# Softmax reads and a softplus MLP on one core: the reads of six batches joined in three pairs, with a new order of steps and new homes

## The chip, the cores and the metric

The kernel runs on one core of a Trainium2 chip. The metric is the device time of one execution in microseconds (us); lower is better. The core's engines are TensorE (PE, matrix products; PEld is its weight load), VectorE (DVE), ScalarE (ACT) and GpSimdE (POOL, all but unused here). SyncE (SP) issues nearly all DMAs. Each engine takes its instructions in the order in which the program gives them, and a wait holds back all that stands behind it on that engine.

## The reference

```python
B, H, S, Ns, D = (8, 8, 512, 32, 64)
...
    scores = scale * np.matmul(x, state.transpose(0, 1, 3, 2))
...
    xread = np.matmul(a, state)        # a = softmax(scores)
    scores2 = scale * np.matmul(state, x.transpose(0, 1, 3, 2))
...
    sread = np.matmul(a2, x)           # a2 = softmax(scores2)
    return np.concatenate([xread, sread], axis=2).astype(np.float32)
...
    x = np.ascontiguousarray(attn_out.transpose(0, 2, 1, 3)).reshape(B * S, H * D)
...
    h = x @ w_in                       # 512 -> 2048
    g = np.maximum(h, 0.0) + np.log1p(np.exp(-np.abs(h)))
    return (g @ w_out).astype(np.float32)
```

Each of 8 batches and 8 heads has 512 rows x and 32 rows state, 64 wide. The x rows read the states (xread) and the states read the x rows (sread). The 8 x 544 rows that come out, 512 wide, go through a two-layer MLP with a softplus between.

## The kernel before

The program is a graph of named steps. Each has an engine or a choice of two, inputs, outputs and a function that emits its instructions. `PLAN` is a long table with one entry for each step, `name:engine:homes`, and is walked from its first entry to its last: it sets the order on every engine and the place of every tile. Engine letters are T (TensorE), A and C (ScalarE), V and W (VectorE) and S (a DMA queued on SyncE). Homes are numbers of PSUM banks (0 to 7) or of pages in one SBUF arena; a new tile in a page waits until the last work on the old tile is done, and where that is a store to DRAM, until the store has landed.

The steps that matter here, b being the batch:

- **Reads, `B.R…`** (function `read`): `sread` of a batch before its division by the row sums. 32 small products in tiles of 128 x 32 with 64 columns (64 records in the trace, for each is two), from `aT.b`, the transposed exponentials (four loads `Le.b.0` to `.3` from the DRAM buffer `te`), and `x.b` (two loads `Lx.b.0` and `.1` of 512 KB from `in_xn_dram`), into the PSUM tile `rp.b`. Behind it come the scaling `X.b`, a transpose `T.b` on TensorE (tile `tp`) and a split into two tiles that only the very last batch of states needs. All other large products use the whole array, in tiles of 128 x 128.
- **First product of the MLP, `h.b.f`**: for batch b and 128 of the 2048 columns, six products of 512 columns (L335, tile `h`). Softplus on ScalarE follows (`s…`, L717).
- **Second product**: for batch 0 plain, `m.0.f.c` (L335, tile `acc`, three products of 512 columns each); for the others in a form with fewer products, `p.b.s.u.j`, with banks `pk_X`, `pk_Y`, `pk_Z` (L764, six products of 256 columns to a step) and `pk_Q`, `pk_W` (L760 and L761).
- **Splits**: every operand is a sum of a high and a low part. ScalarE casts the high part (`wh`, `gh`, `vh`, L316) and VectorE subtracts for the low part (`wl`, `gl`, `vl`, L332). The w_out tiles for `m.0.f` are built from a load `Lo.f` by `ch.o f` on ScalarE (L367 or L369), `cu.o f` and `cr.o f` on VectorE (L374, L377, L382), and then split into `wh.f` and `wl.f`.
- **Spills**: softplus tiles of later batches are stored to `td` in DRAM (`Td…`, 512 KB) and loaded back (256 KB). SyncE issues these among the loads.

`GROUPS` names what one step of TensorE takes in a visit. The engine changes its tile shape where such a step begins and ends, 28 visits in small tiles in all, eight of them reads:

```python
    for name in GROUPS:
        parts = [{"V": states, "Q": scores, "R": read, "K": stacked}[u[0]](*map(int, u[1:].split("."))) for u in name.split("+")]
        op("B." + name, "T", list(dict.fromkeys(t for p in parts for t in p[0])), [t for p in parts for t in p[1]],
           lambda e, parts=parts: [p[2]() for p in parts])
```

Of the kernel before, what the change touches and what calls it, by code (L numbers as in the profile page):

```python
# [19 lines left out]
B, H, S, NS, D = 8, 8, 512, 32, 64  # L20
# [13 lines left out]
GROUPS = ('Q0', 'Q1', 'V1.0', 'V0.1+V1.1', 'V0.2+V1.2', 'V0.3+V1.3', 'Q2+Q3', 'V2.0+V3.0', 'V2.1+V3.1', 'V2.2+V3.2', 'V2.3+V3.3', 'K0.0', 'K0.1', 'K0.2', 'K0.3', 'K1.0', 'K1.1', 'K1.2', 'K1.3', 'K2.0', 'K2.1', 'K2.2', 'K2.3', 'K3.0', 'K3.1', 'K3.2', 'K3.3', 'Q4', 'Q5', 'Q6', 'Q7', 'R0', 'R1', 'R2', 'R3', 'R4', 'R5', 'R6', 'R7')  # L34
# [11 lines left out]
Lt.0.0:S:54 Lt.0.1:S:60 Lz.0:S:71 B.Q0:T:7,2 qk.0.0:A:86 qk.0.1:V:43 w.0:T:0 w.1:T:0 A.0.0:T:7 A.0.1:T:1 Li.0.0:S:56 ch.0.0:A:55 cu.0.0:V:66 cr.0.0:V: M.0.0:V:  # L46
M.0.1:V: Ms.0.0:V:28 Li.0.1:S:82 Lt.1.0:S:10 Lz.1:S:87 Lt.1.1:S:12 Ms.0.1:V:50 cu.0.1:V:0 m.0.0:A: ch.0.1:A:74 m.0.1:A: Lo.1:S:2 Li.0.2:S:24 Lo.0:S:8
Li.0.3:S:32 N.0.0:V: cr.0.1:V: w.2:T:0 w.3:T:0 B.Q1:T:7,2 V.0.0.0.1:T:4,5 V.0.0.0.0:T: Nm.0.0:V: qk.1.0:A:68 ch.o1:A:45 qk.1.1:A:41 A.1.0:T:6 D.0.0:T:1
A.1.1:T:3 N.0.1:V: Nm.0.1:V: D.0.1:T:2 vf.0.0:A:26 vf.1.0:A:64 ch.0.2:A:94 ac.0.1:A:63 ac.0.0:V:21 h.0.1.0:T:7 h.0.0.0:T:0 h.0.1.1:T: h.0.0.1:T: cu.o1:V:10
cr.o1:V: wh.1:A:96 ch.o0:A:34 ch.0.3:A:3 s.0.1:A:4 cu.0.2:V: M.1.0:V: cr.0.2:V: cu.0.3:V: cu.o0:V:79 cr.0.3:V: cr.o0:V: M.1.1:V: Ms.1.0:V:20 V.0.0.1.0:T:  # L50
V.0.0.1.1:T: vf.1.1:V: Ms.1.1:V:45 wl.1:V: vf.0.1:A: B.V1.0:T:1,2 s.0.0:A:46 gh.0.1:A:28 wh.0:A:50 gh.0.0:A:30 h.0.2.0:T:7 h.0.2.1:T: vh.1.0.0:A:52 s.0.2:A:32
Lo.2:S:54 Li.2.3:S:6 Li.1.1:S:60 Lo.3:S:8 ch.o2:C:38 gh.0.2:A:76 Li.1.2:S:82 Sq.1.1:S: Li.1.0:S:18 Lz.2:S:56 Li.1.3:S:24 Li.2.0:S:88 Li.3.2:S:14 Li.2.2:S:34
Li.2.1:S:92 Sq.0.1:S: Li.3.1:S:40 wl.0:V: gl.0.1:V: gl.0.0:V: h.0.3.0:T:3 h.0.3.1:T: s.0.3:A:12 cu.o2:W:69 gl.0.2:V: cr.o2:V: cu.o3:V:85 vl.1.0.0:V: m.1.0:A:
# [905 lines left out]
```

## Time and profile before

| | |
|---|---|
| median of 3 runs | 614.17 us (613.66 to 614.19) |
| the profiled execution | 615.17 us, of which its span 613.4 us and 1.77 us outside it |
| TensorE busy | 604.7 us (99% of the span) |
| VectorE busy | 517.6 us (84%) |
| ScalarE busy | 377.8 us (62%) |
| DMA | 141.04 MB, 230 GB/s mean |
| TensorE's granted clock | 1.00 in every slice |

The span is the time from the first to the last instruction that the profiler recorded; the time of the whole execution lies a little above it. A row of the timeline gives a start, a time, an engine, a line of the program, and how many instructions of one kind follow each other without a gap. TensorE's products overlap: each starts before the one ahead has ended, so the spacing of starts tells more than the duration.

### The profile page before, as it was taken

The page shows a single profiled execution, that of the slowest core. Times are in us where ns is not written, and L with a number is a line of the kernel's source. Part 1 is how long each engine was busy: PE and PEld are TensorE (multiplying, and loading weights), DVE is VectorE, ACT ScalarE, POOL GpSimd, SP SyncE. Part 2 cuts the span into 40 slices and gives each one's busy share as a digit, 9 for nine tenths or more (in the row PEclk, how much of TensorE's full clock was granted, in tenths as well). Part 3 has the DMA queues.
Part 4 walks back from the last instruction along what each step waited for, and adds up shares of the span by engine and source line. Part 5 has one row for each costly group of instructions (what it writes and reads, how often), then busy time and mean ns, then how long its engine had stood idle before and what let it go on. Part 6 is the DMA issues. An engine that isn't in the chain of part 4 may idle for free.

```text
span 613.4 us, 12010 instructions
## 1 busy us (share of the span) xinstructions
PE 604.7 (99%) x4452; PEld 519.5 (85%) x4452; DVE 517.6 (84%) x1117; ACT 377.8 (62%) x631; POOL 0.7 (0%) x6
## 2 busy tenths in 40 slices
PE   7999999999999999999999999999999999999997
PEld 4577667578878989999889998999988899999997
DVE  4999699788799999989699987899785788888974
ACT  4989798898576558674655644465444544546431
POOL 0000000000000000000000000000000000000000
PEclk9999999999999999999999999999999999999999
DMA  8977589988756877988896897874737782441303
GB/s 335 330 279 280 208 294 341 339 274 319 228 179 224 257 254 243 288 260 302 277 311 220 234 294 249 252 252 149 220 123 232 236 287 91 136 155 52 87 2 104
DMA packets 71418, 141.04 MB, mean 230 GB/s; under 512 B 7360, under 2 KB 17600, under 8 KB 71360
## 3 DMA queue, kind: packets, MB, share of 16 engines
q1 hardware_dynamic: 71072, 139.62, 68.7%
q8 instruction: 35, 0.57, 0.4%
q10 hardware_dynamic: 288, 0.66, 0.3%
q14 instruction: 23, 0.19, 0.1%
HBM read 83.10 MB, written 57.15 MB: 229 GB/s over the span
## 4 chain that ended last, share of the span: by engine, by line
PE 71%; DVE 3%; DMA 1%; ACT 1%; SPq 1%; issue 0%; ACTq 0%
PE h L335 14%; PE pk_X L764 14%; PE pk_Y L764 14%; PE pk_Z L764 7%; PE pk_Q L760 4%; PE h L818 2%; PE pk_Q L761 2%; PE pk_W L760 2%; PE pk_Z L760 2%; PE acc L335 1%; PE rp L335 1%; DMA td<-arena 1%; PE h L819 1%; PE pk_Z L761 1%; PE pk_W L761 1%; DVE arena L332 1%
## 5 line engine op out<-in xcount | busy, mean ns | idle before, releaser
L316 ACT CAST arena<-arena 128x896 fp32r<-128x896 f32 (+2 forms) x255 | 186.9, 760 | 137.1 <-DVE arena L745 27.3
L332 DVE TENSOR_TENSOR arena<-arena,arena 128x896 fp32r<-128x896 f32 (+2 forms) x255 | 212.8, 856 | 52.1 <-ACT arena L316 50.6
L335 PE MATMUL h<-arena,arena 128*128 128x512 f32 x760 | 187.0, 397 | 0.0
L335 PEld LDWEIGHTS h<-arena,arena 128*128 128x128 f32 x760 | 139.1, 188 | 38.2 <-issue 4.9
L764 PE MATMUL pk_X<-arena,arena 128*128 128x256 f32 x720 | 103.3, 284 | 0.0
L764 PE MATMUL pk_Y<-arena,arena 128*128 128x256 f32 x720 | 103.1, 283 | 0.0
L764 PEld LDWEIGHTS pk_X<-arena,arena 128*128 128x128 f32 x720 | 93.7, 190 | 4.0 <-issue 0.8
L764 PEld LDWEIGHTS pk_Y<-arena,arena 128*128 128x128 f32 x720 | 93.7, 190 | 3.5 <-issue 0.8
L717 ACT ACTIVATE arena<-h 128x512 f32<-128x512 f32 x112 | 64.4, 601 | 21.1 <-PE h L335 17.2
L764 PE MATMUL pk_Z<-arena,arena 128*128 128x256 f32 x360 | 52.1, 284 | 0.0
L742 DVE TENSOR_TENSOR arena<-arena 128x256 f32<-128x256 f32 x120 | 48.6, 417 | 2.1 <-DMA arena<-td 1.1
L764 PEld LDWEIGHTS pk_Z<-arena,arena 128*128 128x128 f32 x360 | 47.5, 190 | 1.5
L335 PE MATMUL acc<-arena,arena 128*128 128x512 f32 x192 | 45.7, 393 | 0.9 <-DVE arena L332 0.9
L760 PE MATMUL pk_Q<-arena,arena 128*128 128x512 f32 x112 | 43.9, 400 | 0.0
L335 PEld LDWEIGHTS acc<-arena,arena 128*128 128x128 f32 x192 | 35.6, 188 | 8.8 <-DVE arena L332 1.3
L744 DVE TENSOR_TENSOR arena<-arena 128x128 f32<-128x128 f32 x120 | 33.7, 285 | 1.1
L745 DVE TENSOR_TENSOR arena<-arena 128x128 f32<-128x128 f32 x120 | 32.7, 284 | 1.0
L761 PE MATMUL pk_Q<-arena,arena 128*128 128x256 f32 x112 | 31.4, 281 | 0.0
L332 DVE TENSOR_TENSOR arena<-vp,arena 128x512 fp32r<-128x512 f32 x30 | 20.0, 684 | 6.0 <-ACT arena L316 5.8
L760 PEld LDWEIGHTS pk_Q<-arena,arena 128*128 128x128 f32 x112 | 21.2, 189 | 3.3 <-issue 0.8
L818 PE MATMUL h<-sreadT,arena 128*128 128x512 f32 x64 | 22.8, 393 | 0.0
L760 PE MATMUL pk_W<-arena,arena 128*128 128x512 f32 x56 | 22.1, 398 | 0.0
(104 smaller groups left out, 648.3 us busy)
## 6 DMA issues: line engine op xcount, KB each, us to landing
td<-arena SPq DMA_DIRECT2D x56, 512.0 KB, 4.5
arena<-td SPq DMA_DIRECT2D x112, 256.0 KB, 3.6
arena<-in_w_in_dram SPq DMA_DIRECT2D x16, 512.0 KB, 8.2
arena<-in_w_out_dram SPq DMA_DIRECT2D x16, 512.0 KB, 5.6
vd<-arena SPq DMA_DIRECT2D x32, 256.0 KB, 4.2
arena<-vd SPq DMA_DIRECT2D x64, 128.0 KB, 4.2
arena<-in_xn_dram SPq DMA_DIRECT2D x16, 512.0 KB, 5.4
arena<-in_xt_dram SPq DMA_DIRECT2D x15, 512.0 KB, 5.6
```

Of the source, the lines that this page charges most:

```text
L316: nc.scalar.copy(dst, src)
L332: lambda e: eng(e).tensor_tensor(r(dlo()), src(), dhi(), ALU.subtract))
L335: nc.tensor.matmul(dst, lhs, rhs, start=start, stop=stop)
L717: nc.scalar.activation(t[:, :, 0::3] if i == 0 else t[:, :, 1:3], src.rearrange("p (s c t) -> p s c t", s=2, t=P), AF.Softplus)
L742: op(f"sfa.{k}", "V", t, [f"t.{k}:a"], lambda e, g=blocks: nc.vector.tensor_tensor(g()[:, 0:2], g()[:, 4:7:2], g()[:, 7:8].broadcast_to([P ...
L744: op(f"sfb.{k}", "V", [t[0], f"t.{k}:a"], [f"t.{k}:b"], lambda e, g=blocks: nc.vector.tensor_tensor(g()[:, 2], g()[:, 1], g()[:, 4], ALU.add))
L745: op(f"sfc.{k}", "V", [t[1], f"t.{k}:b"], [f"t.{k}:c"], lambda e, g=blocks: nc.vector.tensor_tensor(g()[:, 3], g()[:, 5], g()[:, 2], ALU.s ...
L760: nc.tensor.matmul(at(bank), g(0), r(wform(u, m)(slice(0, 2))), start=first, stop=False, skip_group_check=True)
L761: nc.tensor.matmul(at(bank)[:, 0:256], g(1), r(wform(u, m)(0)), start=False, stop=True, skip_group_check=True)
L764: nc.tensor.matmul(at(bank)[:, 256 * half:256 * half + 256], g(gi), r(wform(u, m)(wi)), start=first and pi == ps[0] and i == 0, stop=i == ...
L818: nc.tensor.matmul(hb, r(w[:, 0, cs]), r(at("sreadT")[:, :, kt, :]), start=kt == 0, stop=False, skip_group_check=True)
L819: nc.tensor.matmul(hb[:, 0:256], r(w[:, 1, cs]), r(at("sreadT")[:, 0, kt, :]), start=False, stop=kt == 3, skip_group_check=True)
```

## The change

Six of the eight reads are put together in three pairs, so that TensorE takes two batches in one visit in small tiles, and the table of steps is written anew: nearly the whole order, 1,002 engines or homes of some 2,890 entries, and with 2,894 entries where there were 2,897. The code that emits the steps is unchanged.

```diff
-GROUPS = (... 'Q7', 'R0', 'R1', 'R2', 'R3', 'R4', 'R5', 'R6', 'R7')
+GROUPS = (... 'Q7', 'R4+R0', 'R1+R2', 'R5+R3', 'R6', 'R7')
...
 PLAN = """
-Lt.0.0:S:54 Lt.0.1:S:60 Lz.0:S:71 B.Q0:T:7,2 qk.0.0:A:86 qk.0.1:V:43 w.0:T:0 w.1:T:0 ...
+Lt.0.0:S:68 Lt.0.1:S:30 Lz.0:S:12 B.Q0:T:2,7 qk.0.1:V:68 qk.0.0:A:85 w.0:T:0 w.1:T:0 ...
```

What moves is better seen in the order of instructions at three places. In it, a page of the arena reads `arena_` and a running number that is each program's own; x3 is three alike in a row.

**First place, the read of batches 4 and 0.** On TensorE before, the reads of batch 4 (`rp_2666`) stand between products of the MLP, and those of batch 0 (`rp_2907`) stand 48 rows further on:

```order
L764 MATMUL pk_1_Y<-arena_2279,arena_2138 128x256 x3
L335 MATMUL rp_2666<-arena_2391,arena_393 32x64 x2
L335 MATMUL rp_2666<-arena_1572,arena_393 32x64 x2
...
L764 MATMUL pk_1_Z<-arena_1600,arena_2138 128x256 x6
...
L335 MATMUL rp_2907<-arena_2836,arena_393 32x64 x2
L335 MATMUL rp_2907<-arena_1667,arena_393 32x64 x2
```

After the change, with the waits of each instruction, batch 0 (`rp_2748`) follows batch 4 (`rp_2747`) directly; the rows from `h_11` on are what stands between the step `h.4.11` and the pair:

```order
L335 MATMUL h_11_2600<-arena_1966,arena_2014 128x512 x3
...
L335 MATMUL h_13_2723<-arena_1472,arena_1375 128x512 x3
...
L760 MATMUL pk_0_Q<-arena_387,arena_2279 128x512
L761 MATMUL pk_0_Q<-arena_387,arena_2279 128x256
...
L335 MATMUL rp_2747<-arena_1023,arena_2243 32x64 x2
L335 MATMUL rp_2748<-arena_1904,arena_2369 32x64 [waits DMAHW4_49,DMAHW3_49,DMAHW7_49,DMAHW2_49,DMAHW0_49]
L335 MATMUL rp_2748<-arena_1904,arena_2369 32x64
L335 MATMUL rp_2748<-arena_1788,arena_2369 32x64 [waits DMAHW5_49]
```

One visit holds both batches, batch 0's read is earlier in the program, and its third instruction waits for the load of `arena_1788`, the second half of x of batch 0 (`Lx.0.1`). On SyncE the loads for that read stood before like this, its page (`arena_1667`) having held an output tile until then:

```order
L326 DMA out_dram<-arena_1667 128x512 [waits DMAHW4_49,DVE_49]
L326 DMA td_120<-arena_333 128x2x512 [waits DMAHW5_49,Activation_49]
L323 DMA arena_2836<-in_xn_dram 128x1024 [waits DMAHW6_49,PE_49]
L323 DMA arena_393<-te_66 32x8x128 [waits DMAHW7_49]
L323 DMA arena_1667<-in_xn_dram 128x1024 [waits DMAHW4_49,DMAHW1_49,DMAHW0_49]
```

and now like this:

```order
L326 DMA td_119<-arena_1788 128x2x512 [waits DMAHW1_49,Activation_49]
L323 DMA arena_2369<-te_66 32x8x128 [waits DMAHW2_49]
L323 DMA arena_2369<-te_66 32x8x128 [waits DMAHW3_49]
L323 DMA arena_1904<-in_xn_dram 128x1024 [waits DVE_49]
L323 DMA arena_1788<-in_xn_dram 128x1024 [waits DMAHW5_49,DMAHW1_49]
L323 DMA arena_1624<-qd_76 128x512 [waits DMAHW6_49]
```

The page `arena_1788` now holds a softplus tile of batch 4 (the output of `s.4.5.0` and `s.4.5.1`, which follow `h.4.11`) until its store `Td.4.5` (`td_119`) has landed, and only then can the load of x into it start.

**Second place, the w_out tile 12 on ScalarE.** `wh.12` is the cast into `arena_1742` before, which waits for a DMA beside VectorE, and which has a page out of which `Td.3.6` is stored:

```order
L367 ACTIVATE arena_848<-arena_276 128x512 [waits DVE_49]
L316 CAST arena_372<-arena_1667 128x512 [waits PE_49]
L316 CAST arena_1431<-arena_385 128x512 [waits PE_49]
L367 ACTIVATE arena_1572<-arena_215 128x512 [waits DMAHW3_49]
L316 CAST arena_1742<-arena_1734 128x512 [waits DMAHW0_49,DVE_49]
L459 ACTIVATE arena_408<-arena_408 128x512
```

After the change `wh.12` is the cast into `arena_1643`:

```order
L367 ACTIVATE arena_1624<-arena_1758 128x512 [waits DMAHW4_49,DMAHW0_49]
L459 ACTIVATE arena_223<-arena_223 128x512
L316 CAST arena_1648<-arena_1023 128x256 [waits DVE_49,PE_49]
L316 CAST arena_1387<-arena_223 128x512 [waits PE_49]
L316 CAST arena_1643<-arena_192 128x512 [waits PE_49]
L316 CAST arena_1715<-arena_1541 128x256 [waits PE_49,Activation_49]
L316 CAST arena_411<-arena_208 128x512 [waits DVE_49,PE_49]
```

It and `wh.13` (`arena_411`) wait for TensorE and VectorE and for no DMA. The page of `Td.3.6` is taken later by `wh.14`.

**Third place, the start on VectorE.** The first product `acc` needs `wl.0` and `gl.0.0`. Before, these are the subtractions into `arena_365` and `arena_367`:

```order
L458 TENSOR_TENSOR arena_312<-st_0_280,mx 128x512
L320 COPY arena_306<-vp_0_1_264 128x256
L458 TENSOR_TENSOR arena_276<-st_1_290,mx 128x512
L332 TENSOR_TENSOR arena_322<-arena_224,arena_322 128x512
L332 TENSOR_TENSOR arena_365<-arena_333,arena_365 128x512
L332 TENSOR_TENSOR arena_363<-arena_327,arena_363 128x512
L332 TENSOR_TENSOR arena_367<-arena_361,arena_367 128x512
```

After the change they are those into `arena_365` and `arena_363`:

```order
L320 COPY arena_219<-vp_0_0_255 128x256
L593 SCALAR_TENSOR_TENSOR arena_370<-arena_276,arena_225 128x256
L444 TENSOR_REDUCE mx<-st_1_294 128x16
L374 TENSOR_SCALAR arena_179<-arena_349 128x512
L332 TENSOR_TENSOR arena_363<-arena_230,arena_363 128x512
L377 TENSOR_SCALAR arena_375<-arena_347 128x512
L378 TENSOR_SCALAR arena_375<-arena_347 128x512
L332 TENSOR_TENSOR arena_365<-arena_225,arena_365 128x512
L332 TENSOR_TENSOR arena_368<-arena_333,arena_368 128x512
```

The second of the two now has two other subtractions (`wl.1`, `gl.0.1`) and one L458 fewer ahead of it, and the copy `ac.0.0` (128 x 512, L320), which stood further up, went to ScalarE. One L593 and three instructions L374 to L378 (`cu.o3`, `cu.o2`) are new ahead of it.

## Rows read from the trace of the kernel before

**Rows 1.** The page: busy times, and TensorE's line of forty slices (busy tenths).

```profile
PE 604.7 (99%) x4452; PEld 519.5 (85%) x4452; DVE 517.6 (84%) x1117; ACT 377.8 (62%) x631; POOL 0.7 (0%) x6
PE   7999999999999999999999999999999999999997
```

**Rows 2.** Waits of TensorE in the whole span: total us, times, longest.

```profile
PE acc L335 <- DVE arena L332: 0.9, 1, 0.9
PE vp L335 <- DVE arena L382: 0.7, 1, 0.7
```

**Rows 3.** Timeline of TensorE, 225 to 270 us: start, time, instructions.

```profile
229.84 0.88 PE L764 MATMUL pk_X<-arena,arena 128*128 128x256 f32 x6
230.56 0.88 PE L764 MATMUL pk_Z<-arena,arena 128*128 128x256 f32 x6
...
245.42 5.68 PE L335 MATMUL h<-arena,arena 128*128 128x512 f32 x24
...
257.74 0.40 PE L760 MATMUL pk_Q<-arena,arena 128*128 128x512 f32 x1
...
258.09 1.60 PE L764 MATMUL pk_X<-arena,arena 128*128 128x256 f32 x12
...
262.05 0.88 PE L764 MATMUL pk_Z<-arena,arena 128*128 128x256 f32 x6
262.85 1.10 PE L335 MATMUL rp<-arena,arena 128*32 128x64 f32 x64
263.88 0.98 PE L764 MATMUL pk_X<-arena,arena 128*128 128x256 f32 x6
264.70 0.88 PE L764 MATMUL pk_Y<-arena,arena 128*128 128x256 f32 x6
```

**Rows 4.** The tile rp: durations (min/median/max ns), first and last start.

```profile
L335 PE MATMUL rp<-arena,arena x512: 219/219/243, 242.0 to 487.2; 128*32 128x64 f32 x171
```

**Rows 5.** The chain of waits, 140 to 190 us: start, time, what.

```profile
150.63 8.16 DMA td<-arena
158.87 0.63 ACT arena L316
159.52 0.69 DVE arena L332
...
175.29 1.21 DVE arena L332 x2
```

**Rows 6.** Timeline of VectorE, 150 to 185 us, with idle time before.

```profile
159.52 0.69 DVE L332 TENSOR_TENSOR arena<-arena,arena 128x512 fp32r<-128x512 f32 x1 [3.29 <-ACT arena L316]
```

**Rows 7.** Timeline of TensorE, 173 to 182 us.

```profile
172.74 2.88 PE L335 MATMUL acc<-arena,arena 128*128 128x512 f32 x12
176.55 4.83 PE L335 MATMUL acc<-arena,arena 128*128 128x512 f32 x20 [0.93 <-DVE arena L332]
```

**Rows 8.** Timeline of TensorE, 0 to 32 us.

```profile
25.50 6.71 PE L335 MATMUL acc<-arena,arena 128*128 128x512 f32 x27
```

**Rows 9.** Timeline of VectorE, 20 to 27 us.

```profile
23.53 2.49 DVE L332 TENSOR_TENSOR arena<-arena,arena 128x512 fp32r<-128x512 f32 x4
25.94 0.46 DVE L377 TENSOR_SCALAR arena<-arena 128x512 uint16<-128x512 uint16 x1
```

**Rows 10.** DMA issues by kind: count, KB each, median us from issue to landing.

```profile
td<-arena SPq DMA_DIRECT2D x56, 512.0 KB, 4.5
arena<-in_w_in_dram SPq DMA_DIRECT2D x16, 512.0 KB, 8.2
arena<-in_xn_dram SPq DMA_DIRECT2D x16, 512.0 KB, 5.4
```

**Rows 11.** Timeline of SyncE's queue, 225 to 265 us.

```profile
255.20 0.33 SPq L323 DMA_DIRECT2D arena<-in_xn_dram  x1
```

**Rows 12.** The page's costliest groups: busy, mean ns of one.

```profile
L717 ACT ACTIVATE arena<-h 128x512 f32<-128x512 f32 x112 | 64.4, 601 | 21.1 <-PE h L335 17.2
```

More of the change, by code (lines that the diff above doesn't have):

```diff
@@ L266 @@
[L266 to L268 removed]
+Lt.0.0:S:68 Lt.0.1:S:30 Lz.0:S:12 B.Q0:T:2,7 qk.0.1:V:68 qk.0.0:A:85 w.0:T:0 w.1:T:0 A.0.0:T:3 Li.0.0:S:32 ch.0.0:A:9 cu.0.0:V:50 cr.0.0:V: A.0.1:T:5 M.0.0:V:
@@ new lines @@
+gl.3.1.3:V: X.3:A:65 gh.3.1.4:A:0 sfb.3.1.5:V: gl.3.1.4:V: sfc.3.1.5:V: N.6.0:V: Nm.6.0:V: p.3.1.2.0:T: p.3.1.2.1:T: T.3:T:5 p.3.1.2.2:T: p.3.1.3.2:T:
+s.5.7.0:A:44 ah.6.1:A:78 s.5.7.1:A: al.6.1:V: p.3.1.3.1:T: p.3.1.2.3:T: p.3.1.4.1:T: p.3.1.4.2:T: p.3.1.3.0:T: p.3.1.3.3:T: p.3.1.4.3:T: gh.3.1.5:A:4
+gl.3.1.5:V: p.3.1.5.3:T: p.3.1.4.0:T: p.3.1.5.2:T: Tr.3.1.7:S:72 Tr.4.0.0:S:86 Lv.6.0.2:S: So.3.0.1:S: Lv.6.0.3:S: Lv.6.1.0:S:26 Tr.4.0.1:S:64 Tr.3.1.6:S:70
+vh.6.0.1:A:12 p.3.1.5.0:T: D.6.0:V:82 ah.6.0:A:28 X.5:A:10 T.5:T:6 vl.6.0.1:V: al.6.0:V: vh.6.0.0:A:14 th.5:A: p.3.1.5.1:T: Tr.4.0.3:S:92 Td.5.7:S:
@@ new lines @@
+e5l.4.1:V: e7l.4.1:V: gl.5.0.1:V: s.7.0.1:A:12 h.7.2:T:7 p.5.0.0.1:T:1 p.5.0.0.3:T:2 p.5.0.1.0:T: p.5.0.1.3:T: p.5.0.0.4:T:4 p.5.0.0.2:T:0 p.5.0.1.4:T:
+p.5.0.1.1:T: gl.5.0.2:V: p.5.0.2.1:T: p.5.0.1.2:T: p.5.0.2.2:T: p.5.0.2.0:T: p.5.0.2.4:T: p.5.0.2.3:T: r.7.1:V: sfa.5.0.6:V: sfb.5.0.6:V: sfc.5.0.3:V:
+sfa.5.0.7:V: Tr.5.1.1:S:64 Tr.5.0.4:S:70 sfa.5.0.4:V: sfb.5.0.4:V: sfc.5.0.4:V: Tr.5.1.2:S:92 Tr.6.0.1:S:28 s.7.1.1:A:72 gh.5.0.3:A:4 s.7.0.0:A: gl.5.0.3:V:
+sfb.5.0.7:V: gh.5.0.5:A:8 s.7.1.0:A: gl.5.0.5:V: sfa.6.0.1:V: p.5.0.3.2:T: p.5.0.3.4:T: p.5.0.3.3:T: gh.5.0.4:A:0 p.5.0.3.1:T: p.5.0.3.0:T: Td.7.0:S:
@@ new lines @@
+Lv.7.1.0:S: Lv.7.1.2:S: Td.7.1:S: Lv.7.2.0:S:78 Tr.5.1.3:S:44 sfc.5.0.7:V: gl.5.0.4:V: sfc.5.0.6:V: gh.5.0.6:A:12 gl.5.0.6:V: gh.5.0.7:A:4 gl.5.0.7:V:
+sfa.5.1.1:V: sfb.5.1.1:V: p.5.0.4.3:T: p.5.0.4.1:T: p.5.0.5.1:T: p.5.0.4.2:T: p.5.0.4.4:T: p.5.0.5.3:T: p.5.0.5.2:T: p.5.0.4.0:T: vh.7.1.0:A:2 vh.7.1.1:A:0
+So.4.1.1:S: Lv.7.2.1:S: Tr.5.1.0:S:18 Tr.5.1.4:S:82 vl.7.1.1:V: sfa.5.1.0:V: sfb.5.1.0:V: sfc.5.1.0:V: sfa.5.1.2:V: sfa.5.1.4:V: vl.7.1.0:V: p.5.0.6.3:T:
+p.5.0.6.2:T: p.5.0.7.2:T: p.5.0.5.0:T: p.5.0.5.4:T: p.5.0.6.4:T: p.5.0.6.0:T: p.5.0.7.0:T: p.5.0.6.1:T: h.7.5:T:7 p.5.0.7.4:T: p.5.0.7.1:T: h.7.4:T:6
@@ new lines @@
+h.8.7.0:T:3 hy.8.7.0:A:56 gh.8.0.1:A:0 hx.8.7.0:V: h.8.6.0:T:6 s.8.0.5.1:A:18 hy.8.6.0:A:57 gl.8.0.0:V: hx.8.6.0:V: h.8.6.1:T:5 h.8.7.1:T:3 gl.8.0.1:V:
+hy.8.6.1:A: sfb.8.0.2:V: hy.8.7.1:A: hx.8.7.1:V: hx.8.6.1:V: s.8.0.6.0:A:92 s.8.0.5.0:A: s.8.0.7.0:A:84 s.8.0.7.1:A: sfc.8.0.2:V: gh.8.0.2:A:8 s.8.0.6.1:A:
+Tr.7.1.0:S:86 Tr.7.1.2:S:28 sfa.8.0.5:V: sfa.8.0.7:V: sfa.8.0.4:V: sfa.7.1.1:V: gl.8.0.2:V: Tr.7.1.7:S:82 Tr.7.1.6:S:56 Tr.7.1.4:S:44 Tr.7.1.3:S:78
+Tr.7.1.5:S:64 p.8.0.0.2:T:7 p.8.0.0.1:T:6 p.8.0.0.3:T:0 p.8.0.0.0:T:3 p.8.0.1.3:T: p.8.0.1.2:T: p.8.0.0.4:T:5 p.8.0.1.1:T: p.8.0.1.0:T: p.8.0.1.4:T:
@@ L269 @@
+e2.7.1:V: e6l.8.0:V: e6.8.0:V: So.8.0.1.3:S: So.8.0.1.1:S: So.8.0.1.2:S: So.8.0.1.0:S: e3.7.1:V: e4.7.1:V: So.7.1.0:S: e5.7.1:V: e7.7.1:V: e6.7.1:V: So.7.1.1:S:
+So.7.1.2:S: So.7.1.3:S:
 """
```

429 lines of the change are left out of this document (205 added, 224 removed).

## The prediction

> **What bounds the kernel now.** I read the page first: TensorE is busy 604.7 us, 99% of a span of 613.4, and its slices are full from the second to the last but one [rows 1]. Only what shortens TensorE's own sequence, or lets it wait less, can move the end. VectorE (84%) and ScalarE (62%) have room on average, so a swap of engine here or there costs nothing unless TensorE waits for that very tile.
>
> The second view is the list of TensorE's waits. One lies outside the start: 0.9 us of the `acc` products for a subtraction of VectorE [rows 2]. The third is the timeline around a read. Six products of 256 columns normally follow each other at 0.72 us (229.84 to 230.56), while those ahead of the read take 0.80, the read 1.03, and those behind it 0.82 [rows 3]. So the reader should see two things that can be won: small-tile visits that cost some tenths each, and one wait of about a microsecond.
>
> The fourth view is the chain that leads to that wait. A store of a softplus tile takes 8.16 us to land from 150.63; the cast `wh.12` starts at 158.87 right behind it, since its page is the one stored; the subtraction starts at 159.52, and VectorE had nothing to do for 3.29 us before it [rows 5, 6]. VectorE stays behind from there, and at 175.29 the subtractions still run for which TensorE waits until 176.55 [rows 5, 7]. The idle time is 0.93. Normally a product of 512 columns lasts 0.39 but the next starts 0.23 later ((5.68 - 0.39)/23 in the 24 products at 245.42 [rows 3]), so TensorE loses 0.93 + 0.16 = 1.09 us.
>
> **The joined visits.** A read has 64 records of 0.219 us [rows 3, 4], so its last one starts at 262.85 + 1.10 - 0.22 = 263.73, and 63 steps in 0.88 us are 0.014 us each. Entering costs 0.80 - 0.72 = 0.08. From the last record to the next large product are 0.15 (263.88 - 263.73), where a further small record would come after 0.014: 0.136 lost. The six products behind take 0.82 in place of 0.72: 0.10 lost. A batch that follows another in the same visit spares all three, 0.08 + 0.136 + 0.10 = 0.32 us. Three joins give 0.95 us. The number of records stays the same, so nothing is added on the other side. Bounds: 0 if the 0.236 us on leaving are paid for each batch's PSUM tile and the 0.08 for each new x, and -0.95. I take -0.95, since the rows show the loss only where the tile shape changes, and 14 ns within.
>
> **The wait at 175 us.** `wh.12` no longer has the page of a store that it must wait for, and neither has `wh.13`. If VectorE had its 3.29 us there, its subtractions would run ahead of TensorE instead of 1 us behind. The wait is then gone: -1.09. What is late next are `wl.13` and `gl.0.13` or the tile 15, which stand close ahead of the products that need them; with the 3.3 us back they are early, without it late by about as much as now. `wh.14` now takes a stored page, but far later. Bounds: -1.09 and 0 (the wait only moves).
>
> **The start.** The first 27 `acc` products take 6.71 us where 26 x 0.23 + 0.39 = 6.37 would do: 0.34 us, since the low part that the second product needs ends at 23.53 + 2.49 = 26.02, half a microsecond behind the first product [rows 8, 9]. In the new order two subtractions, an L458 and a copy fewer stand ahead of the later of the two operands, each about the 0.60 at which subtractions follow each other ((2.49 - 0.69)/3), so 2.4 us less, and four smaller instructions more, at most 0.46 each by the nearest row [rows 9], so 1.8 more. The operand comes at least 0.6 us sooner, and the 0.34 go. Other waits of the start are as large as 0.7 [rows 2], and the fills between them are reordered too: bounds -1.0 and +0.4. I take -0.4, near the wait that I can see go.
>
> **What the new order adds.** The pair of batches 4 and 0 needs x of batch 0 earlier in the program than the single read did, where it stood 48 rows further on, and the second half of it goes into the page of a softplus tile of batch 4. From the end of `h.4.11` two softplus instructions must run (0.60 each [rows 12]), the store must land (4.5), and the load must land (5.4 [rows 10]); with 0.3 for the hops between, that is 0.3 + 1.2 + 4.5 + 5.4 = 11.4 us. TensorE has until then eight steps of six products of 256 columns at 0.72, three steps of `pk_Q` at 0.35 (257.74 to 258.09 [rows 3]), three steps `h` of six products at 0.23, and batch 4's reads with 0.98: 5.76 + 1.05 + 4.14 + 0.98 = 11.9 us. The load is half a microsecond early at the medians. Before, a page of an output tile was waited for, and the load, issued at 255.20 [rows 11], was due at 260.6, 2.2 us ahead of the read. Queued on SyncE behind the new wait are a load from `qd`, two output stores and loads from `td`, which have spare time there; behind the read on TensorE stands everything.
>
> So this term is between 0 and, with the slow store (8.16 [rows 5]) and a load as slow as the median of `in_w_in_dram`, the slowest kind of that size (8.2 [rows 10]), 17.9 - 11.9 = 6.0 us. The other two pairs have about 1 to 1.5 us at the same medians. I take +0.6 for all three together: the margin of 0.5 is small beside the 3.7 between the median store and the slow one, so a wait at the first pair is about as likely as none, and would mostly be about a microsecond.
>
> The Trainium skill, "DMA: Bandwidth & Descriptors", section "Anatomy of one DMA — SWDGE (gpsimd) path", fits one DMA as about 2.0 us and its bytes over 436 GB/s, though for DMAs of another queue; by that an estimate of 3.2 us each for store and load would leave the pair 4.0 us of room, with a sum that is 0.6 us lower. The medians of this trace, 4.5 and 5.4, are longer, and the measurement decides.
>
> Totals on the other engines barely change: a few dozen steps swap between VectorE and ScalarE in both directions, hidden behind a TensorE that is never idle from 26 to 610 us but for the one wait. Without that cover a step of VectorE costs its 0.60 us. The tail after the last product is in the same order.
>
> **Sum.** -0.95 - 1.09 - 0.4 + 0.6 = -1.84 us. The profiled span of 613.4 becomes 611.56, with the 1.77 outside it 613.3. The profiled execution was 1.00 us above the median of the runs shown (615.17 and 614.17), so for a median run I predict 614.17 - 1.84 = 612.3 us. A change under 0.2% (1.23 us) can't be told from none here.
>
> **Rivals.**
>
> *The waits only move.* The joins are certain to shorten TensorE's sequence, but the time that VectorE or a DMA was late at 175 us and at the start turns up at `m.0.13`, at a pair, or elsewhere. For it speaks that leads of 0 to 1 us are the rule in this program; against it, that only two places of before show TensorE waiting after the start has settled. Time: 614.17 - 0.95 = 613.2, within 0.2%. Chance 0.27.
>
> *The pair waits for x of batch 0* (the other side). Place: the third record of batch 0's read, behind the store and the load in one page. With a wait of w the time is 614.17 - 0.95 - 1.09 - 0.4 + w = 611.7 + w. It is slower than before by over 0.2% when w passes 3.7 us, that is when store and load together take 4.2 us more than their medians; at 6.0 it would be 617.7. For it speaks the store of 8.16 [rows 5], against it that such a store is nearly twice the median of 56 [rows 10]. Chance 0.12.
>
> In the Trainium skill, "TensorE: Matmul & The Clock Gate", section "Part 3: Packing small matmuls — row/col tiling", matmuls keep strict program order, so by that page a late operand of the second batch would hold all that follows, as this rival says; the trace agrees in that nothing of TensorE ran in the 0.93 us at 175 us.
>
> *The joins spare nothing*, if the loss belongs to each batch: 614.17 - 1.09 - 0.4 + 0.6 = 613.3. Included with the waits that only move, about 0.05 of its 0.27.
>
> **Range and chances.** My forecast has 0.61 and by its own terms lies between 614.17 - 3.04 = 611.1 (the start at its lower bound, no new wait) and 611.7 + 1.5 = 613.2 (1.5 us of waits at the pairs). The range: downward 611.1 with another 0.2 for the spread of the medians, 610.9; upward it takes in the waits that only move and a wait of about 3 us at the pair, 614.9. Faster by over 0.2%: 0.57 of the forecast and 0.05 of the moved waits, 0.62. Within 0.2%: 0.04 + 0.22 + 0.02 = 0.28. Slower: 0.10.
>
> **What would show it.** Right: the first visit with 128 rp records in about 1.9 us, in three such visits; no idle time of `acc` products near 175 us and no VectorE hole of 3 us near 156; the `acc` products at 25 us without a lost 0.34. Wrong: rp records with an idle time whose releaser is a DMA from `in_xn_dram`; a wait for VectorE L332 at another `acc`; TensorE's first `acc` later than 25.5; or a visit of two batches that takes 2.06 us, twice a single one.

## The result, and the profile after

The change makes the kernel slower: 618.07 us (615.12 to 620.48 in 8 runs) against 614.10 us of the kernel before (613.61 to 615.50 in 8 runs), a ratio of 1.006 with a 95% interval of 1.0033 to 1.0086. Forecast were 612.3 us and a faster kernel, with the range ending at 614.9. The profiled execution took 619.43 us, with a span of 617.6, 4.2 us over that of the kernel before. One execution of all that follow, the profiled one of run k4 (844.72 us), had a mean granted clock of 0.656 and is left out.

The page of the changed kernel answers to [rows 1]; the third line is TensorE's granted clock in forty slices, the last a DMA queue (its packets, its MB, and their share of the time):

```profile
PE 606.7 (98%) x4452; PEld 521.5 (84%) x4452; DVE 515.8 (84%) x1116; ACT 377.3 (61%) x633; POOL 0.7 (0%) x6
PE   7999999999999999999999998999999999999997
PEclk9999999999999999999999998999999999999999
q8 instruction: 35, 0.57, 0.4%
```

The reader is to see that TensorE is as full as before, but for one slice in which the clock dips too; the totals of the other engines hardly move. The waits of TensorE (answering to [rows 2]; total, times, longest in us) say more:

```profile
PE vp L335 <- DVE arena L382: 2.5, 1, 2.5
PE sc L335 <- DMA arena<-in_xt_dram: 1.9, 1, 1.9
...
PE pk_Y L764 <- issue: 1.0, 1, 1.0
...
PE vq L335 <- DVE arena L332: 0.4, 1, 0.4
```

The wait of `acc` for L332 is gone, as forecast. Three others have come or grown (`vp` waited 0.7 us before [rows 2]), and none of them is the wait at a pair of reads that I had named as the rival.

**At the start.** Before, TensorE's waits between 10 and 14 us were two, of 1.3 and 0.7 us:

```profile
11.41 1.82 PE L335 MATMUL sc<-arena,arena 64*32 64x512 f32 x16 [1.32 <-DVE arena L458]
13.98 0.67 PE L335 MATMUL vp<-arena,arena 64*32 64x256 f32 x16 [0.75 <-DVE arena L382]
```

Now they are one. The timeline of TensorE, with idle time in brackets (the last row answers to [rows 8]):

```profile
8.99 0.88 PE L613 MATMUL wp<-ident 128*128 128x128 f32 x4
12.41 0.64 PE L335 MATMUL vp<-arena,arena 64*32 64x256 f32 x8 [2.54 <-DVE arena L382]
13.01 1.96 PE L335 MATMUL sc<-arena,arena 64*32 64x512 f32 x16
...
26.54 7.42 PE L335 MATMUL acc<-arena,arena 128*128 128x512 f32 x30
```

The first states (`vp`) stand ahead of the scores of batch 1 (`sc`) now, so both wait for VectorE's conversion. The first `acc` product starts at 26.54, 1.04 us later than before, and the 0.34 us behind it that I expected to go are still lost (7.42 where 29 x 0.23 + 0.39 = 7.06 would do: 0.36). The table by stretches (start:end, length, busy times, then granted clock, DMA share, GB/s) shows a second price, at the start and again at 382 us:

```profile
10.00:13.00 3.00, 0.59 (x8) 0.15 (x8) 3.00 (x7) 0.90 (x3) 0.00 (x0) 0.99 1.00 385
13.00:17.00 4.00, 4.00 (x37) 1.90 (x34) 3.72 (x9) 2.52 (x6) 0.00 (x0) 0.58 1.04 414
378.00:382.00 4.00, 2.10 (x24) 0.84 (x22) 2.64 (x6) 1.17 (x3) 0.00 (x0) 0.95 0.59 181
382.00:385.00 3.00, 3.00 (x21) 2.91 (x14) 1.25 (x2) 2.01 (x3) 0.00 (x0) 0.50 1.01 290
```

Behind each of the two longest holes the granted clock falls to 0.50 of full speed, the lower of its two levels (1.2 GHz), for 3.4 us of the record. The first begins half a microsecond after work has resumed.

**At the pair of batches 1 and 2.** The timeline there:

```profile
299.19 2.01 PE L335 MATMUL rp<-arena,arena 128*32 128x64 f32 x128
301.13 0.98 PE L764 MATMUL pk_X<-arena,arena 128*128 128x256 f32 x6
301.94 0.40 PE L764 MATMUL pk_Y<-arena,arena 128*128 128x256 f32 x2
303.36 0.73 PE L764 MATMUL pk_Y<-arena,arena 128*128 128x256 f32 x4 [1.01 <-issue]
```

The joined visit itself is as forecast: 128 records and 1.94 us to the next product, where two visits took 2 x 1.03 [rows 3]. But a step of six products breaks off after two and goes on 1.42 us later, where 0.24 would do: 1.18 us lost, and no operand is named. That such a wait splits a step whose six products have the same operand tile is the first hint that it isn't an operand.

**At 380 us.** The chain of waits, and SyncE's queue:

```profile
370.55 2.47 PE h L335 x11
373.02 7.69 DMA arena<-in_xt_dram
380.71 0.14 issue
380.85 1.16 PE sc L335 x9
```

```profile
367.56 4.88 SPq L323 DMA_DIRECT2D arena<-td  x3
372.50 0.42 SPq L323 DMA_DIRECT2D arena<-te  x1
373.02 0.40 SPq L323 DMA_DIRECT2D arena<-in_xt_dram  x1
```

The load of x transposed for batch 7 (`Lt.7.0`) is issued at 373.02, behind a spill load that waited for its page, and lands 7.69 us later; TensorE waits 1.9 us for it. Behind it the timeline shows the lower clock at work:

```profile
382.10 1.65 PE L764 MATMUL pk_X<-arena,arena 128*128 128x256 f32 x6
383.54 1.48 PE L764 MATMUL pk_Z<-arena,arena 128*128 128x256 f32 x6
384.82 0.96 PE L764 MATMUL pk_X<-arena,arena 128*128 128x256 f32 x6
385.62 1.55 PE L335 MATMUL h<-arena,arena 128*128 128x512 f32 x6
```

Three steps take 3.52 us in place of 2.16: 1.36 lost.

Against the profiled execution of before this adds up to +1.04 (start), +1.18 (303 us), +1.90 and +1.36 (380 us), -1.09 (175 us) and -0.95 (joins): +3.44 of the 4.2. Where the rest is isn't shown: the list of waits has no other that is longer than before, apart from 0.1 us at the start.

### The profile page after: what moved, and what is told of

It reads as the page before. It is cut to its first block, busy times and chain, and to the rows that moved or that the text cites. A ratio compares the mean times of both kernels' runs of the same rounds, so it can differ in the third digit from the quotient of the medians.

```text
span 617.6 us, 11987 instructions
## 1 busy us (share of the span) xinstructions
PE 606.7 (98%) x4452; PEld 521.5 (84%) x4452; DVE 515.8 (84%) x1116; ACT 377.3 (61%) x633; POOL 0.7 (0%) x6
## 4 chain that ended last, share of the span: by engine, by line
PE 92%; DMA 3%; DVE 2%; ACT 1%; issue 1%; SPq 0%; ACTq 0%; DVEq 0%
PE h L335 27%; PE pk_X L764 14%; PE pk_Y L764 13%; PE acc L335 7%; PE pk_Z L764 7%; PE pk_Q L760 4%; PE h L818 2%; PE vp L335 2%; PE pk_Q L761 2%; PE pk_Z L760 2%; PE pk_W L760 2%; PE vq L335 2%; PE sc L335 1%; DMA arena<-in_xt_dram 1%; PE h L819 1%; PE rp L335 1%
## 5 line engine op out<-in xcount | busy, mean ns | idle before, releaser
L332 DVE TENSOR_TENSOR arena<-arena,arena 128x896 fp32r<-128x896 f32 (+2 forms) x255 | 214.0, 858 | 61.3 <-ACT arena L316 58.8
L332 DVE TENSOR_TENSOR arena<-vp,arena 128x512 fp32r<-128x512 f32 x30 | 20.1, 685 | 6.4 <-ACT arena L316 6.4
```

The source lines that it names most:

```text
L332: lambda e: eng(e).tensor_tensor(r(dlo()), src(), dhi(), ALU.subtract))
```

## The experiments

Times are medians, each with the kernel before on the same chip beside it, and the 95% interval of the ratio. A profile is one execution; its waits of 0.2 us or less are left out.

| run | median us (runs) | ratio to before | first acc at, in the profile | waits of TensorE after 30 us in the profile: where it goes on, and how long it idled |
|---|---|---|---|---|
| the changed kernel | 618.07 (8) | 1.0033 to 1.0086 | 26.54 | 303 us: 1.0; 381: 1.9 |
| k2, the same again | 618.85 (6) | 1.0037 to 1.0081 | 26.45 | 305: 1.5; three of 0.3 to 0.5 |
| e1, load for batch 7 earlier | 618.91 (4) | 1.0047 to 1.0086 | 26.34 | 273: 2.1 |
| e2, start reordered | 616.57 (10) | 1.0019 to 1.0053 | 25.57 | 303: 1.2 |
| e3, pair 1+2 apart | 615.13 (7) | 1.0013 to 1.0046 | 26.38 | none |
| e4, pair 1+2 earlier | 618.25 (4) | 1.0044 to 1.0074 | 26.32 | 303: 0.6; 381: 1.5 |
| f1, start with other banks | 618.04 (4) | 1.0038 to 1.0077 | 25.57 | 272: 1.4; 305: 1.7; 405: 0.7 |
| f2, three things mended | 615.12 (11) | 1.0006 to 1.0024 | 25.69 | 271: 0.8 |
| f3, and all pairs apart | 615.65 (11) | 1.0012 to 1.0034 | 25.57 | none |
| f4, f2 and a fourth place | 615.64 (10) | 1.0008 to 1.0027 | 26.68 | 277: 0.4; 496: 0.6 |
| k1, instructions shifted | 615.52 (12) | 0.9998 to 1.0029 | 26.75 | 494: 0.3; 516: 0.6 |
| k3, start, load, shift, all joined | 613.84 (12) | 0.998 to 1.000 | 25.32 | none |
| k4, k3 with all pairs apart | 615.16 (11) | 1.0003 to 1.0024 | left out | left out |
| h1, before with a store earlier | 614.28 (11) | 0.9992 to 1.0010 | 25.14 | 67: 0.8 |
| h2, before again | 614.58 (1) | one run | 25.59 | 176: 0.3 |
| g1, before, reads done twice | 621.85 (1) | one run | 25.26 | 265: 0.3 |
| k5, before, instructions shifted | 614.62 (11) | 0.9993 to 1.0011 | 25.45 | none |

The wait of 0.4 us of `vq` at 90 us is in all of them, before as after, and is left out.

### First: one thing at a time in the changed kernel

**e1.** One entry of the table moves:

```diff
+Lt.7.0:S:0
 Tr.4.0.5:S:18 Le.6.3:S:92
-Lt.7.0:S:0
```

> The changed kernel with one DMA moved: the second load of x transposed for batch 7 stands ahead of a spill load on SyncE's queue that waits 3.6 us for its page, instead of two entries behind it. Theory (late load, then a lower clock): the wait of 1.9 us at the scores of batch 7 goes or falls under 0.5, and with it the 3.4 us at half clock behind it (1.7 us); the profiled span falls from 617.6 by 3 to 4 us to about 614, with the waits at the start and at 302 us left as they are. Rival (the load is slow by contention, not late in the queue): it starts 2.8 us sooner but lands no more than 1 us sooner, and the span falls by 1 us at most.

The wait at 381 us is gone from the profile (span 614.8), but the median isn't lower. A spilled tile that came back late cost 2.1 us at 273 us in its stead. Of the other profiles in which `Lt.7.0` stands where the change put it, e3, f1, k1 and k2 don't show that wait, e2 shows 0.2 us of it and e4 1.5. So the load is late by over a microsecond in some executions, two of these seven, and mending it alone can't be told in the median.

The runs of the changed kernel point the same way. Four of the eight took 615.1 to 616.7 us, with a mean granted clock of 0.997, and four 619.4 to 620.5, with 0.994. The profiled one, with its two falls of the clock, is of the second kind. The median of 618.07 lies in the gap between the two, so it can move by more than one cause is worth.

**e2.** The start in the order of before:

```diff
-Lt.1.1:S:80 Lt.1.0:S:56 Lz.1:S:65
+Lt.1.0:S:56 Lz.1:S:65 Lt.1.1:S:80
...
-V.0.0.0.1:T:6,0 B.Q1:T:5,4
+B.Q1:T:5,4 V.0.0.0.1:T:6,0
```

> The changed kernel with the start in the order of the kernel before: the loads for the scores of batch 1 in the order first half, zf, second half, and those scores ahead of the first states on TensorE. Theory (one long hole of 2.5 us at 9.9 us lets the clock fall): the hole becomes two of about 1.3 and under 1 us, the clock stays at 1.00 in the first 30 us, and the first acc product, at 26.5 in the changed kernel, comes at 25.5 to 26.0; the span falls by 0.5 to 1.0 us. Rival (the subtractions and copies of VectorE and ScalarE set the start, not TensorE): the first acc product stays within 0.2 us of 26.5.

The first `acc` came at 25.57, 0.97 earlier, as the theory had it, but not by its way: the hole was still one, of 2.8 us, because the scores wait for VectorE to finish with a PSUM bank (5) that the new homes give them. The clock stayed at 1.00 in this profile. The median falls by about 1.5 us against 618.07, though the intervals of the two ratios overlap.

**e3.** The pair of batches 1 and 2 apart, in `GROUPS` and in the table:

```diff
-'R1+R2'
+'R1', 'R2'
...
-B.R1+R2:T:1,3
+B.R1:T:1
...
-h.5.8:T:6
+h.5.8:T:6 B.R2:T:3
```

> The changed kernel with the pair of batches 1 and 2 taken apart: batch 2 is read 54 matmuls later, behind h.5.8. Theory (the 256 instructions of a double visit empty TensorE's supply of instructions, which the 16 KB instruction transfers fill): the idle 1.0 us at 303 us goes, and no transfer of instructions follows the one before it by more than 320 instructions there; the join's 0.3 us is lost; net -0.8 to -0.9 us. Rival (the products of pk_Y wait for an operand or a bank that the trace doesn't name): the idle time in front of the second two products of p.2.1.7.1 stays.

The idle time at 303 us is gone, and 2.9 us of the median with it, more than the 0.9 that the theory gave; with so few runs the intervals of the two ratios overlap. One sign that I had named didn't come: a transfer of instructions there still follows the one before it by 399 instructions, not by 320 at most. That the wait is gone is shown, its price isn't.

**e4.** Joined, but elsewhere (`B.R2+R1:T:3,1` ahead of `p.2.1.6.0`, four steps earlier):

> The changed kernel with the pair of batches 1 and 2 still joined, but batch 2 first, and four steps (44 matmuls or 24 and their weights) earlier in the order, so that the visit stands elsewhere against the transfers of instructions. Theory (instruction supply, a matter of where in a block of 256 instructions the visit begins): the idle 1.0 us behind the visit goes or shrinks under 0.5 and the span falls by about 1.1. Rival (a double visit always empties the supply, or the wait belongs to p.2.1.7.1): it stays at 1.0 us or more.

The wait with no operand named is gone here too. Others took its place (0.6 us for VectorE behind the visit, 1.5 for `Lt.7.0`), so the median says nothing on it.

### Second: is the idle time behind a double visit the supply of instructions?

TensorE's instructions come in blocks. The page of the changed kernel, above, shows 35 transfers on q8. TensorE has 8,993 instructions (2 x 4,452 on PE and PEld, and 89 of semaphores and the like), so one transfer brings 257. The trace has the time of each. In the runs with a double visit of batches 1 and 2 in the place of the change, and in g1:

```
kernel            visit starts   transfer starts, lands   TensorE goes on   idle
changed kernel       299.19        301.10  301.98            303.36         yes
the same again (k2)  299.84        302.19  303.11            304.54         yes
e2                   298.20        300.15  301.07            302.55         yes
f1                   300.15        302.73  303.60            305.05         yes
e1                   301.57        302.05  302.93               -           no
g1, batch 0          262.81        262.61  263.58            265.06         yes
```

In each of the five with idle time TensorE goes on 1.38 to 1.48 us after the transfer has landed, and has issued 250 to 275 instructions since the visit began. A visit of two batches issues 256 instructions in 1.9 us, where the rest of the kernel takes some 18 us for as many (35 blocks in 613 us). In e1, TensorE was two microseconds later for another reason, the transfer came 0.5 us into the visit, and nothing idled.

The place of the stop says more. Counted from the start over all instructions of TensorE in the trace, the four stops behind batches 1 and 2 come after 4,289 of them, each time the same, and the one in g1 after 3,777: 512 apart, exactly two blocks of 256. So each stop is where a new block begins. Take every such place, 256 instructions apart, in the 17 profiles other than k4's, and the time from the landing of its transfer to the instruction behind it. It is never below the 1.38 to 1.48 us of the five stops. In e1 it is 1.52, so the block was there just in time; at the same place it is 2.5 in e3 and 5.0 in k1, and in the kernel before it is 5.9 or more everywhere. At the other two pairs of the changed kernel such a place lies inside the visit, but its transfer had landed 2.4 us or more before the visit began, and nothing idled. What makes a transfer start when it does stays open.

**g1** doubles the visits of the kernel before:

```diff
-            for g in range(2):
+            for g in (0, 1, 0, 1):
```

> The kernel before with every read done twice within its visit (the second time over the first, same result): eight visits of 128 records and 256 instructions, at eight places in the blocks of instructions, with no load or order changed. Theory (a visit of 256 instructions can empty the supply): TensorE idles 0.5 to 1.5 us, with no operand named, in or just behind one to four of the eight visits, and the transfers of instructions around these start over 60 instructions later than usual. Rival (the idle time at 303 us of the changed kernel was an unnamed operand or bank): eight visits of 1.9 to 2.0 us and no such idle time; the span grows by 8 x 0.9 = 7.2 us.

One of eight visits idled, the fewest that the theory allowed, and the 0.26 us are less than its 0.5. Nor did the transfer start late, as I had expected: it began 0.2 us ahead of the visit. The timeline of g1 there:

```profile
262.81 1.99 PE L335 MATMUL rp<-arena,arena 128*32 128x64 f32 x126
265.06 0.27 PE L335 MATMUL rp<-arena,arena 128*32 128x64 f32 x2 [0.26 <-issue]
```

TensorE stops two records before the end of a visit all of whose operands are there and in use. An operand or a bank can't be the cause in the middle of it.

**k1** moves the place in the blocks, by small products where TensorE waits:

```diff
             nc.tensor.matmul(at("h.idle")[:, 0:P], idle, idle, start=True, stop=True)
+        for i in range(16):
+            nc.tensor.matmul(at("h.idle")[NS * (i % 4):NS * (i % 4) + NS, 0:D], idle[:, 0:NS], idle[:, 0:D], start=True, stop=True)
```

> The changed kernel with 16 small products more (32 records, 64 instructions) on idle data right behind the warming products, where TensorE waits for its first loads anyway; order, waits and pairs are those of the changed kernel, only the place of every later instruction in the blocks of TensorE's instruction transfers is 64 sooner. Theory (instruction supply): the transfer that came late beside the double visit of batches 1 and 2 now comes ahead of it, no idle time with no operand named stands behind that visit, and the median falls by 1 to 3 us below that of the changed kernel measured beside it. Rival (that idle time costs nothing in most executions, or is no matter of instructions): the median stays within 0.5 us of it.

**k2** is the unchanged kernel beside it:

> The changed kernel, unchanged, on this chip, as the measure for the run beside it and for a second profile. Both theories: a median of 616.5 to 619; the first acc product at 26.3 to 26.6 with a hole of over 2 us before 12.5. By the theory of instruction supply about 1 us idle at 302 us again; by the theory of late loads waits of 1 to 2 us at one or two places of 270, 380 and 400 us, not the same as in the first profile.

k1 is at 615.52 and k2 at 618.85 on the same chip, and the timeline of k1 at the pair has no idle time:

```profile
299.34 2.01 PE L335 MATMUL rp<-arena,arena 128*32 128x64 f32 x128
301.28 0.98 PE L764 MATMUL pk_X<-arena,arena 128*128 128x256 f32 x6
302.10 0.88 PE L764 MATMUL pk_Y<-arena,arena 128*128 128x256 f32 x6
```

while k2 idled 1.5 us there again, and had small waits elsewhere, none of the 1 to 2 us that I had given for late loads:

```profile
PE pk_Y L764 <- issue: 1.5, 1, 1.5
...
PE pk_Z L761 <- DVE arena L332: 0.5, 1, 0.5
...
PE pk_X L764 <- DVE arena L771: 0.4, 1, 0.4
```

The transfers of k1 start at 294.77 and 302.97, one well ahead of the visit at 299.34 and one behind it. So it is the supply of instructions: sixty-four instructions at a place where TensorE waits anyway, 300 us earlier, take the idle time away, and the median is 3.3 us lower. Of these the profiles show 1.2 to 1.9 us as lost behind the visit; where the rest goes stays open. The runs of both kernels spread over 4 us (614.03 to 617.89, and 616.01 to 620.43), so a part of the 3.3 may lie in which executions were met.

**k5** puts the same products into the kernel before:

> The kernel before with only the 16 small products. Theory (they help by the place of the double visits in the instruction blocks, and the kernel before has none): the median stays within 0.3 us of the kernel before. Rival (they help in another way, by the start or the clock): it falls by 0.5 us or more here too.

614.62 against 614.45 beside it: in a kernel without double visits the sixteen products bring nothing, which speaks against the start or the clock as the way by which they help.

The Trainium skill, "Runtime: NRT & Kernel Launch", section "Instruction fetch mechanics", states that instructions come in blocks of 16 KiB, 256 each, fetched ahead while the block at hand is executed, and that crossing a boundary is "mostly hidden". The transfers here agree (0.57 MB in 35), and the 8 single visits of the kernel before do as well. At the double visit of batches 1 and 2 it is not hidden: 1.0 to 1.7 us idle in four profiles of the five in the table.

### Third: was there 1.09 us to win at 175 us?

**h1** moves one store of the kernel before:

```diff
-Sv.2.2.0:S: Sv.1.3.1:S: Sv.3.3.0:S: Td.3.6:S:
+Td.3.6:S: Sv.2.2.0:S: Sv.1.3.1:S: Sv.3.3.0:S:
```

> The kernel before with one store moved: the spill Td.3.6, whose page wh.12 waits for, stands ahead of three spills of states on SyncE's queue and starts 3.3 us sooner; nothing else is changed. Theory (the 1.09 us at 175 us belong to the one profiled execution, which was 1.0 us above the median; most executions of the kernel before don't have them): the median stays within 0.3 us of the kernel before, and the profile shows no wait of acc at 175 us. Rival (the prediction's term: the wait is in every execution and goes with the store's delay): the median falls by 0.8 to 1.1 us.

**h2** is the kernel before, profiled again:

> The kernel before, unchanged, profiled a second time. Theory (the wait at 175 us is one execution's): no wait of the acc products over 0.3 us after 30 us, VectorE's hole at 156 us under 2.5 us, span near 612.5. Rival: the same 0.9 us of idle time at 175 us, span 613 to 613.5.

h1's profile has no wait of `acc` (it has one of 0.8 us at 67 us, for ScalarE), and its median is the kernel's of before, 614.28 against 614.19. In h2 the wait is 0.29, as its timeline shows beside [rows 7]:

```profile
172.62 3.11 PE L335 MATMUL acc<-arena,arena 128*128 128x512 f32 x13
176.01 4.83 PE L335 MATMUL acc<-arena,arena 128*128 128x512 f32 x20 [0.29 <-DVE arena L332]
```

and in g1 and k5, which up to there are the kernel before (k5 with its sixteen products at the start), it doesn't appear. The chain that leads to it is in every one of them, though. In h2 the store took even longer than the 8.16 us of [rows 5], and the hole of VectorE, for which I had expected under 2.5 us, is nearly that of [rows 6]:

```profile
148.35 9.92 DMA td<-arena
```

```profile
159.00 0.69 DVE L332 TENSOR_TENSOR arena<-arena,arena 128x512 fp32r<-128x512 f32 x1 [2.66 <-ACT arena L316]
```

In g1 and k5 the hole is 2.22 and 2.12 us. So VectorE's hole behind that cast is in all four, and only what arrives of it at TensorE, 0.93, 0.29 or nothing, differs from one execution to the next. What could be won in the median is within h1's interval, 0.5 us faster to 0.6 slower.

### Fourth: all together, and what a join is worth

**f1** gives the scores of batch 1 free banks besides (`B.Q1:T:2,4`):

> The changed kernel with its start mended further: besides the loads and the scores of batch 1 ahead of the first states, these scores take two PSUM banks that nothing reads any more (2 and 4 for 5 and 4), since in the earlier trial they waited for VectorE to finish with bank 5. Theory (holes of TensorE at the start, and the lower clock behind them): the scores start at 10.6 to 11.4 us, no hole is over 1.6 us, the clock stays at 1.00, and the first acc product comes at 25.2 to 25.9 against 26.5; the median falls about 1 us below that of the changed kernel. Rival (VectorE and ScalarE set the start): the first acc stays at 26.2 or later, whatever the scores do.

The scores now start at 11.03, the longest hole is 1.2 us, and the first `acc` at 25.57; the start's theory holds in this profile. The median, of four runs, isn't 1 us lower, as I had expected; its profile shows the double visit's 1.7 us and waits of 1.4 and 0.7 us for late operands.

**f2** is f1, e1's edit and e3's edit together; **f3** takes the other two pairs apart too:

> The changed kernel with all three mended: the start as in the trial with banks, the load of x transposed for batch 7 earlier, and batches 1 and 2 read in two visits. Theory (the loss against the kernel before is the start with its lower clock, the late load with its lower clock, and the idle time behind the double visit): what is left of the forecast, 614.2 - 1.09 (no wait at 175 us) - 0.64 (two joins) and 0 to -0.4 at the start, 612.0 to 612.6, faster than the kernel before. Rival (the order is fragile in many places, each execution waits somewhere else): profile and times still show waits of 1 to 3 us for operands loaded from DRAM, and the median stays at 614 or above.

> The same with all three pairs taken apart, batch 4 one step (2 matmuls) ahead of batch 0 and batch 5 one step (6 matmuls) ahead of batch 3, so that only the joins differ. Theory (a join spares 0.32 us): 0.64 us slower than with two joins, 11 visits of the array in small tiles more alike to before, and each read again with 0.08, 0.15 and 0.10 lost around it. Rival (a join spares nothing, the loss belongs to each batch): the same time within 0.2 us.

f2 gets back 2.9 of the 4 us but is still 0.06 to 0.24% slower than the kernel before, where I expected it to be faster; the rival was right that waits remain. Its chain shows what kind:

```profile
261.97 6.56 DMA arena<-td
268.54 0.02 issue
268.56 0.44 DVE arena L742
...
270.05 1.01 DVE arena L332
271.06 0.04 issue
271.11 0.38 PE pk_Q L761
```

A spilled tile is loaded back late, three steps of VectorE wait for it, and behind them a subtraction that TensorE wants.

**f4** puts that subtraction ahead of the three:

```diff
-sfa.2.1.1:V: gh.2.0.7:A:12 sfb.2.1.1:V: sfb.2.1.2:V: sfc.2.1.1:V: sfa.2.1.0:V: gl.2.0.7:V:
+gh.2.0.7:A:12 gl.2.0.7:V: sfa.2.1.1:V: sfb.2.1.1:V: sfb.2.1.2:V: sfc.2.1.1:V: sfa.2.1.0:V:
```

> The mended kernel with a fourth place: gh.2.0.7 and gl.2.0.7, for which TensorE waited 0.8 us at 271 us in its profile, stand ahead of the three steps on VectorE that wait for a spilled tile to come back. Theory (late spill loads of the new order hold VectorE, and TensorE behind it): no wait at 271 us, and the median falls by 0.4 to 1.0 us below that of the mended kernel (615.1), to the kernel before or below it. Rival (that wait too is one execution's, with others of its kind elsewhere): the median stays within 0.3 us of 615.1.

The rival was right: that wait is gone, others stand at 277 and 496 us, and the median is no lower. Its first `acc` comes at 26.68, with the start of f1 and f2: in this execution the first scores take 1.96 us, where f2's take 1.09. So the start, too, isn't mended in every execution.

**k3** is f1, e1's edit and the 16 products, with all pairs joined; **k4** the same with all pairs apart:

> The changed kernel with the start mended, the load for batch 7 earlier, all three pairs joined, and the 16 small products. Theory (all three causes found, and a join spares 0.32 us): 0.3 us faster than the mended kernel with batches 1 and 2 apart (615.1), 614.6 to 615.0, so about as fast as the kernel before. Rival (double visits lose time in another way too): 616 or above.

> The mended kernel with the 16 small products and all three pairs taken apart; beside the one with all three joined (613.84) only the joins differ, and neither profile should show idle time for instructions. Theory (a join spares 0.32 us): 0.95 us slower than that, about 614.8. Rival (a join spares nothing once no supply is emptied): within 0.3 us of 613.84.

k3 is better than forecast: 613.84 against 614.49 beside it, a ratio of 0.998 to 1.000. It has the lowest median here, though its interval reaches that of no difference. Its waits of TensorE are nearly all at the start:

```profile
PE sc L335 <- DMA arena<-in_zp_dram: 1.3, 2, 0.8
PE ab L429 <- DVE arena L468: 1.3, 1, 1.3
...
PE pk_X L764 <- DVE arena L771: 0.2, 1, 0.2
```

k4 is 1.3 us slower than k3, on another chip, with 0.95 forecast, and their intervals don't overlap; f3 is 0.5 slower than f2 with 0.64 forecast, and theirs do. So the joins do spare time, though these medians don't give the size. The timeline of f3, where one step of `pk_Q` stands between the reads of batches 4 and 0, does:

```profile
247.18 1.10 PE L335 MATMUL rp<-arena,arena 128*32 128x64 f32 x64
248.21 0.50 PE L760 MATMUL pk_Q<-arena,arena 128*128 128x512 f32 x1
...
248.76 1.10 PE L335 MATMUL rp<-arena,arena 128*32 128x64 f32 x64
249.79 0.50 PE L760 MATMUL pk_Q<-arena,arena 128*128 128x512 f32 x1
```

From the first read to what follows the second are 2.61 us, of which the step takes 0.35 [rows 3]; joined it is 1.94 (as at 299.19 above). One join spares 2.61 - 0.35 - 1.94 = 0.32 us. The other two weren't measured apart.

## Why the prediction was wrong

- **The joins.** The size was right, 0.32 us each. The step that failed is the sentence behind it: "The number of records stays the same, so nothing is added on the other side." The records stay, their pace doesn't: 256 instructions follow each other without the slower products between, and at one of the three pairs the next block of instructions came too late. This cost 1.2 to 1.9 us behind the visit in four profiles, and it is the part that gives back most of the median when it is mended by itself (2.9 us in e3, 3.3 in k1).
- **The wait at 175 us** (-1.09) was that large in one execution only. The chain that led to it was read rightly and recurs (h2), but the sum took from the median what TensorE lost in the profiled execution alone. The warning was on the table: that execution was 1.00 us above the median, which I noted and then treated as an offset.
- **The start** (-0.4) came out at +1.0. I priced the two subtractions that the first `acc` waits for and didn't follow TensorE's own order there: the states ahead of the scores, behind a conversion, turned two short holes into one of 2.5 us. The profiles of e2 and f1 have the 1.0 back; f4's, with f1's start, hasn't.
- **What the new order adds** (+0.6 at the pairs). No pair waited: `rp` has no wait in any profile of the changed kernel. The mechanism, a load queued on SyncE behind one that waits for its page, was the right one, but it struck where I hadn't looked, at the scores of batch 7 and at spilled tiles, in one execution here, in another there. In the profiled execution the scores of batch 7 cost most of all, 1.90 + 1.36 = 3.26 us with the lower clock behind them, and the sum has no term for either.
- **The rivals.** The waits that only move came nearest (chance 0.27), but by it no wait could grow, and the time was 613.2. The rival on the slower side named the wrong place. The supply of instructions was in none of the cases. Nor would the range, which ended at 614.9, have held with that alone: e3 and k1, without the idle time behind the visit, are at 615.13 and 615.52.
- **A row misread.** The prediction counts one wait of TensorE outside the start, and calls TensorE never idle from 26 to 610 us but for it. There is a second, 0.38 us of `vq` at 89 us; it is in every profile alike and changes nothing in the sum.

## What to carry to other kernels

Count the instructions of a burst and not only its time: where 256 instructions pass in 1.9 us, the stream of instructions can be the bound, and whether it is depends on where in a block the burst begins and on how early the next transfer starts (in e1 the same burst at the same place lost nothing). Before a wait in a profile is entered as a gain, see that the profiled execution stands at the median, or profile twice. See also whether the times of a kernel fall into groups, as a median between two groups moves easily. A new order has to be walked on each engine from its first row, and above all where TensorE has no cover yet.

## What the runs showed of the hardware that I had not expected

- A transfer of a block of TensorE's instructions takes 0.9 to 1.0 us in these five cases, and the engine goes on 1.38 to 1.48 us after it has landed. In none of the 17 profiles other than k4's did it enter a block sooner than that.
- The granted clock fell to 0.50 for 3.4 us after holes of 2.2 to 2.5 us at the start (in the changed kernel, its repeat k2, e1, e3, e4 and k1) and of 1.9 us at 381 us, but not after one of 2.8 us in e2, nor after 2.1 us at 273 us in e1; before each fall TensorE had been idle or in small tiles.
